# Ordering VectorE's copies behind GpSimd's DMA issues in a planned attention and MoE kernel

## The chip, the cores and the metric

The kernel runs on one core of one Trainium2 chip. The metric is the device time of one execution in microseconds (us). The kernel before takes 302.99 us, the median of three runs (302.73 to 303.19).

The engines are named as in the profile: PE is TensorE, with PEld for its weight loads; ACT is ScalarE; DVE is VectorE; POOL is GpSimd; SP is SyncE, which issues DMAs only. GpSimd issues DMAs too.

## The reference

Sliding-window attention over 8 batches, 8 heads, 576 positions and 64 dimensions, followed by one gated feed-forward layer over the 4608 tokens that come out of it.

```python
scores = scale * np.matmul(q, k.transpose(0, 1, 3, 2))
rel = pos[:, None] - pos[None, :]
mask_plain = (rel >= 0) & (rel < 32)                         # heads 0 to 3
mask_dil = (rel >= 0) & (rel < 32 * 4) & (rel % 4 == 0)      # heads 4 to 7
...
attn_out = np.matmul(attn, v)                                # (8, 8, 576, 64)
x = attn_out.transpose(0, 2, 1, 3).reshape(4608, 512)
h = x @ w_in                                                 # w_in: 512 x 2048
g = h * (1.0 / (1.0 + np.exp(-beta * h)))
out = g @ w_out                                              # w_out: 2048 x 512
```

## The kernel before

**The work.** Tokens go through the feed-forward layer in nine tiles of 512. For a tile t, `slot_h` makes one "slot" for each of 16 column blocks of w_in: four matmuls of 512 columns into one PSUM bank (L887), a tanh on ScalarE (L896) and a gate on VectorE that writes `g` (L901). In tile 0, the first four slots are taken apart, so that the halves of x can come at different times. `block` then makes the output of 128 tokens from 16 matmuls against w_out in four parts of four (L922), an evacuation on ScalarE or VectorE (L937, L939) and a store by SyncE (L942).

**Attention** runs batch by batch, between the slots and blocks of the tile before. q and k of the first three batches are loaded into `st` (L394) and transposed on TensorE (L469 for the dilated heads, L479 for the plain ones), and copied out of PSUM (all copies have line L243). From batch 3 on, GpSimd casts them to DRAM and SyncE's DMA transposes bring them in (L460). Scores of the dilated heads are L683, of the tail L652, of the plain heads L747 (L711 from batch 3). ScalarE takes the exponentials (L619) into `ptd`, `ptt` and `pt`; these are multiplied by a mask (L623) on VectorE or GpSimd, except in batch 0, whose masks are added on TensorE (L673, L733, L736). Values are L788 (dilated), L773 (tail) and L804 (plain); VectorE normalises them (L638, L639) into `xdm`, `xdt` and `xsp`. The result is transposed into `xT`, the input of the slots, on TensorE for batches 0 and 1 (L841, L826, L856) and by SyncE's DMA transposes from batch 2 on (L514, L519, L506, L533).

**SBUF copies with a choice of engine.** `halo` fills the first rows of `vp`; `mixed` makes `dkt` out of `dk`; `padded` makes `qt` out of `dq`; `spread` brings v into `vd`. Their deps and engines are given to `plan.op` with an estimated time for each engine.

**What sets the order.** The kernel schedules itself. Every step is an `Op` with the engines that may run it, a time for each, its deps, a due time `vt` and, where it needs PSUM, a `Group` that takes one of eight banks. `Plan.run` keeps a clock for each engine, picks the next op by estimated start and due time, and emits it; so each engine's queue is fixed before the kernel runs, and on the chip each engine works it off in order, waiting on semaphores. `NUDGE` shifts the estimated start of single ops, by their number, in the choice alone. `CAPS` bounds the banks of one kind. Ops that are flagged `sbuf` keep the estimated times of VectorE and GpSimd apart, since they go from SBUF to SBUF:

```python
if o.sbuf:
    at = {e: max(t, port["DVE" if e == "POOL" else "POOL"]) for e, t in at.items()}
```

Where TensorE would be without work by the plan for more than 170 ns (300 ns early on) and a bank is free, `filler` puts a matmul of zeros there (L1035):

```python
if filler is not None and s <= filler_until and free["PE"] + (300 if free["PE"] < COLD else 170) < s:
```

The masks of the plain heads (`mask_n`) and of the dilated heads (`mask_d`), the identities `ident_b` (for the transposes) and `ident_f` (for beta), and `add_d` are made on GpSimd at the head of its queue, among its DMA issues.

Of the kernel before, what the change touches and what calls it, by code (L numbers as in the profile page):

```python
# [17 lines left out]
class Group:  # L18


    def __init__(self, kind):
        self.kind, self.bank, self.users = kind, None, []
        self.read = {}


class Op:
    def __init__(self, engs, fn, deps, vt, acquire, group, dma, lat, halves=False, sbuf=False):
# [12 lines left out]
class Plan:  # L40
# [3 lines left out]

    CAPS = {"h": 3, "p": 4, "o": 2, "z": 4, "a": 8, "s": 5, "w": 6}
    SWITCH = 95
    NUDGE = {9: -400, 35: 400, 78: -150, 90: 150, 103: -900, 156: -900, 164: -60, 191: -60, 208: 150,
        220: 900, 247: -400, 251: 60, 266: -150, 268: -150, 270: -150, 326: 900, 376: 400,
        397: 900, 420: 900, 432: -900, 490: 900, 525: 150, 545: 60, 554: 900, 562: -60, 571: 60,
        574: 150, 1103: -400, 1113: 400}  # L50
    LAT = {"PE": 210, "ACT": 45, "DVE": 45, "POOL": 60, "SP": 0}
    NEAR = {"PE": 40, "ACT": 60, "DVE": 60, "POOL": 60, "SP": 0}

    def __init__(self, banks):
        self.ops, self.banks = [], banks

    def op(self, engs, fn, deps=(), vt=0.0, acquire=None, group=None, dma=0, lat=None, halves=False, sbuf=False):
        acquire = acquire if acquire is None or isinstance(acquire, list) else [acquire]
        o = Op(engs, fn, deps, vt, acquire, group or acquire, dma, lat, halves, sbuf)
        o.bias = self.NUDGE.get(len(self.ops), 0)  # L60
        self.ops.append(o)
        return o

    def run(self, filler=None, filler_until=0.0):
# [12 lines left out]
        n_held = {k: 0 for k in self.CAPS}  # L77
        ends = []
        halves = False
        port = {"DVE": 0.0, "POOL": 0.0}  # L80

        def release(now):
# [18 lines left out]
        while n_left:  # L101
            best = None
            near = {}
            for o in avail:
                base = o.ready
                at = {e: max([free[e], base] + [t for x, t in o.group.read.items() if x != e]
                             if o.group is not None and e != "PE" else [free[e], base]) for e, d in o.engs}
                if o.sbuf:
                    at = {e: max(t, port["DVE" if e == "POOL" else "POOL"]) for e, t in at.items()}
                fin = min(at[e] + d for e, d in o.engs)  # L110
                for e, d in o.engs:
                    start = at[e]
                    if start + d > fin + 100:
                        continue
                    if o.dma and len(lanes[e]) >= 8:
                        start = max(start, lanes[e][-8])
                    if o.acquire is not None:
                        start = bank_at(o.acquire, start)
                        if start is None:
                            continue  # L120
                    near.setdefault(e, []).append((start, o, d))
            picks = []
            for e, c in near.items():
                first = min(s + o.bias for s, o, _ in c)
                s, o, d = min((x for x in c if x[0] + x[1].bias <= first + self.NEAR[e]), key=lambda x: (x[1].vt, x[0]))
                picks.append((s, o.vt, e, o, d))
            assert picks, "no work can start"
            s, _, e, o, d = min(picks, key=lambda x: (x[0], x[1]))
            if filler is not None and s <= filler_until and free["PE"] + (300 if free["PE"] < COLD else 170) < s:
                now = free["PE"]  # L130
                open_banks = {x.bank for x in held.values()}
                spare = [b for b, t in bank_free.items() if b not in open_banks and t <= now]
                if spare:
                    filler(max(spare, key=lambda b: -bank_free[b]))
                free["PE"] = now + (225 if now < COLD else 115)
                halves = False
# [48 lines left out]
def kernel(  # L185
# [34 lines left out]
    DIRECT = 3  # L220
# [21 lines left out]
    def copy(e, out, in_):  # L242
        (nc.scalar.copy if e == "ACT" else E[e].tensor_copy)(out=out, in_=in_)  # L243
# [134 lines left out]
    mask_ops = {}  # L378

    def late_mask(key, ns, fn, vt):  # L380
        mask_ops[key] = plan.op([("POOL", ns)], fn, vt=vt, sbuf=True)
# [25 lines left out]
    def first_keys():  # L407
# [3 lines left out]
                      ap=[[RD * D, 2 * GD], [2 * S * D, 2], [1, RD * D]])  # L411
        o = load("SP", (stage, src), [], -9.1, 576, .41, 400, 1200)
        return [plan.op([("ACT", 175 + .834 * RD * D), ("DVE", 160 + 1.042 * RD * D)],
                        lambda e, x=x: copy(e, std[0][:, x], stage[:, x]), [o], -9.1, sbuf=True) for x in range(2)]

    def direct_vp(b, deps, vt):

# [2 lines left out]
        for hs in ((slice(0, 4),) if b else (slice(0, 2), slice(2, 4))):  # L420
# [5 lines left out]
            def halo(e, hs=hs):  # L426
                copy(e, rows[0:WIN, hs, 1:NI, 0:D], rows[QT:P, hs, 0:NI - 1, 0:D])
            out.append(plan.op([("DVE", 160 + .27 * n * 320), ("POOL", 170 + 1.04 * n * 320)], halo, [o],
                               b - 1 if b else -2.5, sbuf=True))
        return out  # L430

    def direct_vd(b, deps, vt, tdeps=()):
# [104 lines left out]
    def attention(b, ld, names, vts):  # L537
# [43 lines left out]
        o = plan.op([("DVE", 450), ("POOL", 550), ("ACT", 500)], mixed,  # L581
                    (steps["KD0"] + steps["KD1"] if b < DIRECT else ready["D"][0:1]) + war(("dkt", kv)), vt_of["T"] - .01, sbuf=True)
        used(("dk", kv, 0), o)
        used(("dk", kv, 1), o)
        wrote(("dkt", kv))
# [1 line left out]
        for c in range(2):  # L587
            def padded(e, c=c):
# [2 lines left out]
                     dq[kv][rows, :, :, P:].rearrange("p r h u -> p (r h) u"))  # L591
            o = plan.op([("DVE", 250), ("POOL", 500), ("ACT", 290)], padded,
                        (steps["QD0"] + steps["QD1"] if b < DIRECT else ready["D"][1:]) + [fill1] + war(("qt", kv)),
                        vt_of["T"] - .01, sbuf=True)
            used(("dq", kv, 0), o)
            used(("dq", kv, 1), o)
            tail_ready.append(o)
# [7 lines left out]
        def spread(e):  # L605
            copy(e, vd[kv][:, :, :, 0:D], vd16_of[b])
        o = plan.op([("POOL", 1100), ("DVE", 620), ("ACT", 1030)], spread,
                    [ld["vd"][0], (fill3, fill4)[kv]] + war(("vd", kv)), vt, sbuf=True)
        used("vd16" if b < DIRECT else ("st", kv), o)
        wrote(("vd", kv))  # L610
        vdeps["D"] = [o]
# [4 lines left out]
        def exp_and_mask(key, sop, g, vt, n, sc, w, m, tiles):  # L616
# [4 lines left out]
            if b >= ADDED or key == ("T",):  # L621
                def mask(e):
                    E[e].tensor_tensor(out=w(), in0=w(), in1=m(), op=ALU.mult)  # L623
                ex = plan.op([("POOL", 170 + 2.2 * n), ("DVE", 160 + .8 * n)], mask,
                             [ex] + [mask_tail if key == ("T",) else mask_ops["D" if key[0] in (2, 3) else "n"]],
                             vt, sbuf=True)
            wrote(*tiles)
            sdone[key] = ex

# [439 lines left out]
```

## Time and profile before

| | |
|---|---|
| median of three runs | 302.99 us (302.73 to 303.19) |
| the profiled execution's own time | 302.73 us |
| its span | 301.0 us |
| granted clock of TensorE | 0.999 |
| zero matmuls | 67 |
| first w_in matmul (L887) / first w_out matmul (L922) | 17.92 / 37.26 us |
| DMA | 41.98 MB, mean 139 GB/s |

The profile is of one execution. Its busy shares are means over a head of 18 us in which batch 0 is brought up, a middle up to some 92 us in which attention and the feed-forward layer mix closely, and a rest in which TensorE goes from one group of matmuls to the next. In the timeline, a row merges instructions that follow each other on one engine; the first number is its start, the second its length, both in us, and a bracket at its end holds the engine's idle time before it with what ended it. Rows that begin a new group of matmuls can overlap the last of the group before, because the drain of a matmul is counted in. In the table of windows, an entry is the busy time of an engine in that stretch with the number of instructions in brackets.

### The profile page before, as it was taken

The numbers are of one execution on the slowest core, as the hardware profiler recorded it, in microseconds if no ns is written. First come the engines' busy times: TensorE is split into PE (matmuls) and PEld (weight loads), VectorE is DVE, ScalarE is ACT, GpSimd is POOL, SyncE is SP. The second block draws the span as 40 slices with busy tenths as digits, with TensorE's granted clock in tenths as the row PEclk, the third lists the DMA queues.
The fourth block names the chain that finished last, engine by engine and source line by source line (L and its number), as shares of the span: only waits on it lengthen the run. The fifth ranks groups of instructions, "written<-read, shape, count | busy, mean of one in ns | idle before, by whom it ended". The sixth has DMA issues, their size and how long they took to land.

```text
span 301.0 us, 6071 instructions
## 1 busy us (share of the span) xinstructions
PE 295.5 (98%) x2344; PEld 150.4 (50%) x2344; DVE 187.5 (62%) x424; ACT 172.2 (57%) x311; POOL 83.9 (28%) x121
## 2 busy tenths in 40 slices
PE   8999999999999999999999999999999999999995
PEld 5866546444554445544444544444454444444454
DVE  4769787798857846887677647865772363343300
ACT  3868764867745744667484548454852654554311
POOL 8997324764236006400730074000000000000000
PEclk9999999999999999999999999999999999999999
DMA  8999999899889998999899979993124100100122
GB/s 164 188 210 201 206 178 222 122 133 145 196 188 197 158 199 173 199 158 191 145 172 158 224 146 173 179 211 90 37 74 117 70 1 35 37 35 35 59 82 70
DMA packets 111248, 41.98 MB, mean 139 GB/s; under 512 B 87620, under 2 KB 104596, under 8 KB 111220
## 3 DMA queue, kind: packets, MB, share of 16 engines
q0 software_dynamic: 60336, 18.58, 59.5%
q1 hardware_dynamic: 50740, 22.95, 37.8%
q8 instruction: 18, 0.29, 0.4%
q14 instruction: 10, 0.08, 0.1%
q10 hardware_dynamic: 144, 0.07, 0.1%
HBM read 37.76 MB, written 18.87 MB: 188 GB/s over the span
## 4 chain that ended last, share of the span: by engine, by line
PE 94%; DVE 2%; ACT 1%; POOL 1%; issue 1%; POOLq 0%; ACTq 0%
PE bank L922 41%; PE bank L887 40%; PE bank L804 2%; PE bank L1035 2%; PE bank L683 1%; PE bank L788 1%; PE bank L711 1%; PE bank L469 1%; PE bank L747 1%; PE bank L479 1%; ACT ptd L619 1%; PE bank L773 1%; DVE xdm L639 1%; PE bank L673 1%; DVE ptd L623 1%
## 5 line engine op out<-in xcount | busy, mean ns | idle before, releaser
L922 PE MATMUL bank<-w_out_bf,g 128*128 128x512 bf16 (+2 forms) x608 | 140.0, 368 | 0.0
L901 DVE SCALAR_TENSOR_TENSOR g<-tnh,bank 128x512 bf16<-128x512 bf16 x144 | 97.3, 685 | 68.2 <-ACT tnh L896 67.2
L896 ACT ACTIVATE tnh<-bank,beta_half 128x512 bf16<-128x512 f32 x144 | 97.9, 690 | 70.3 <-PE bank L887 63.8
L887 PE MATMUL bank<-xT,w_in_bf 128*128 128x512 bf16 (+1 forms) x584 | 137.0, 376 | 0.0
L887 PEld LDWEIGHTS <-w_in_bf 128*128 128x128 bf16 x584 | 55.7, 98 | 62.8 <-issue 0.3
L922 PEld LDWEIGHTS <-g 128*128 128x128 bf16 x608 | 54.5, 98 | 55.7
L937 ACT ACTIVATE osb<-bank 128x512 f32<-128x512 f32 (+1 forms) x35 | 20.6, 589 | 31.3 <-PE bank L922 30.7
L619 ACT ACTIVATE pt<-bank 128x384 bf16<-128x384 f32 (+1 forms) x54 | 20.8, 467 | 6.8 <-PE bank L711 4.3
L619 ACT ACTIVATE ptd<-bank 128x512 bf16<-128x512 f32 x32 | 16.8, 602 | 6.2 <-PE bank L683 6.2
L639 DVE TENSOR_TENSOR xsp<-bank,rcp 96x384 bf16<-96x384 f32 x32 | 17.7, 554 | 1.3 <-DVE rcp L638 0.2
L623 DVE TENSOR_TENSOR pt<-pt,mask_n 128x384 bf16<-128x384 bf16 (+1 forms) x41 | 14.8, 391 | 5.7 <-ACT pt L619 5.5
L638 DVE RECIPROCAL rcp<-bank 128x4 f32<-128x4 f32 (+2 forms) x72 | 12.8, 178 | 5.5 <-PE bank L804 2.4
L1001 POOL COPY pace<-xT 1x2 bf16<-1x2 bf16 x4 | 0.7, 175 | 51.2 <-DMA xT<-x 51.2
L394 POOL DMA_DIRECT2D vp<-in_v_dram x9 | 14.7, 1632 | 0.4 <-PE bank L469 0.4
L623 DVE TENSOR_TENSOR ptd<-ptd,mask_d 128x512 bf16<-128x512 bf16 x27 | 12.0, 465 | 3.6 <-ACT ptd L619 3.0
L639 DVE TENSOR_TENSOR xdm<-bank,rcp 128x256 bf16<-128x256 f32 x32 | 13.6, 425 | 1.1
L394 POOL DMA_DIRECT2D s<-in_q_dram x10 | 13.5, 1351 | 0.0
L394 POOL DMA_DIRECT2D vt<-in_v_dram x16 | 13.3, 993 | 0.0
L1035 PE MATMUL bank<-zero 128*128 128x256 bf16 x67 | 11.6, 310 | 1.3 <-DVE warm L302 1.1
L394 POOL DMA_DIRECT2D s<-in_k_dram x10 | 11.0, 1100 | 1.4 <-issue 1.1
L804 PEld LDWEIGHTS <-pt 128*128 128x128 bf16 x192 | 8.9, 97 | 4.7
L804 PE MATMUL bank<-vp,pt 128*128 128x65 bf16 x192 | 9.8, 193 | 0.0
(112 smaller groups left out, 172.2 us busy)
## 6 DMA issues: line engine op xcount, KB each, us to landing
out_dram<-osb SPq DMA_DIRECT2D x35, 256.0 KB
s<-in_k_dram POOLq DMA_DIRECT2D x10, 288.0 KB, 7.1
s<-in_q_dram POOLq DMA_DIRECT2D x10, 288.0 KB, 10.0
w_out_bf<-in_moe_w_out_dram POOLq DMA_DIRECT2D x2, 1024.0 KB, 16.5
vp<-in_v_dram POOLq DMA_DIRECT2D x7, 288.0 KB, 17.3
st<-in_q_dram POOLq DMA_DIRECT2D x6, 288.0 KB, 11.1
x<-xsp SPq DMA_DIRECT2D x12, 144.0 KB
st<-in_k_dram POOLq DMA_DIRECT2D x5, 288.0 KB, 13.2
```

Source lines behind the costliest of these rows:

```text
L394: {"POOL": nc.gpsimd, "SP": nc.sync}[queue].dma_start(out=out, in_=in_)
L619: nc.scalar.activation(out=w(), in_=sc(), func=ACT.Exp, scale=SCALE)
L623: E[e].tensor_tensor(out=w(), in0=w(), in1=m(), op=ALU.mult)
L638: nc.vector.reciprocal(out=r, in_=p[..., D])
L639: nc.vector.tensor_tensor(out=dst, in0=p[..., 0:D], in1=r.unsqueeze(len(p.shape) - 1).to_broadcast(list(p.shape[:-1]) + [D]), op=ALU.mult)
L804: nc.tensor.matmul(pv[:, a, h2, :], lhsT=lhs, rhs=vp[kv][:, (2 * x + h2) * NI + 3 * j + a, 0:D + 1], start=True, stop=True)
L887: nc.tensor.matmul(bank(g)[:, a:z], lhsT=w_in_bf[:, kt, fb * P:(fb + 1) * P], rhs=xT[:, kt, xo + a:xo + z], start=(i == 0 and kt == kts[0] ...
L896: nc.scalar.activation(out=th[:, 0:n], in_=bank(g)[:, 0:n], func=ACT.Tanh, scale=beta_half[:, fb:fb + 1])
L901: nc.vector.scalar_tensor_tensor(out=g_t[t % 2][:, fb, c0:c0 + n], in0=th[:, 0:n], scalar=1.0, in1=bank(g)[:, 0:n], op0=ALU.add, op1=ALU.mult)
L922: nc.tensor.matmul(bank(g)[:, lo:hi], lhsT=g_t[t % 2][:, fb, tb * P:(tb + 1) * P], rhs=w_out_bf[:, fb, lo:hi], start=(fb == 0), stop=(fb = ...
L937: nc.scalar.mul(out=ob[:, lo:hi], in_=bank(g)[:, lo:hi], mul=0.5)
L1035: nc.tensor.matmul(BANKS[b][:, 0:256], lhsT=zero[:, 0:P], rhs=zero[:], start=True, stop=True)
```

## The change

In `Plan.run`, an op with the flag `sbuf=2` may start on VectorE, by the plan, only 300 ns after the end of the last DMA issue that GpSimd was given. The flag goes to the four SBUF copies (`halo`, `mixed`, `padded`, `spread`). The masks, the casts of the first keys and the making of the masks keep the old treatment with `sbuf=1`. Two times of VectorE in the plan become shorter: `mixed` 360 instead of 450 ns, and a mask 160 + 0.53 n instead of 160 + 0.8 n. The table `NUDGE` is another one, with 31 entries instead of 29, none of them shared but for the number 90 (-900 instead of 150) and 420 (-400 instead of 900). No op, no dep and no wait is added in the program itself; what differs is the order in which the ops are emitted, the engine that each op with a choice goes to, the bank that it gets and the number of zero matmuls, 58 instead of 67.

```diff
-    NUDGE = {9: -400, 35: 400, 78: -150, 90: 150, 103: -900, 156: -900, 164: -60, 191: -60, 208: 150,
-        220: 900, 247: -400, 251: 60, 266: -150, 268: -150, 270: -150, 326: 900, 376: 400,
-        397: 900, 420: 900, 432: -900, 490: 900, 525: 150, 545: 60, 554: 900, 562: -60, 571: 60,
-        574: 150, 1103: -400, 1113: 400}
+    NUDGE = {3: -900, 11: 150, 16: -400, 32: -400, 37: -400, 48: 900, 61: 150, 90: -900, 115: 900,
+        155: -150, 195: -400, 240: 900, 293: -150, 323: -400, 333: 400, 354: -150, 360: 60,
+        365: -900, 374: -400, 402: 400, 420: -400, 540: -900, 542: -400, 546: -150, 547: 400,
+        578: -900, 680: 400, 681: 900, 821: -900, 836: 900, 870: 150}
...
+        issuing = 0.0
         port = {"DVE": 0.0, "POOL": 0.0}
...
+                if o.sbuf == 2 and "DVE" in at:
+                    at["DVE"] = max(at["DVE"], issuing)
                 if o.sbuf:
                     at = {e: max(t, port["DVE" if e == "POOL" else "POOL"]) for e, t in at.items()}
...
             if o.sbuf:
                 port[e] = s + d
+            elif o.dma and e == "POOL":
+                issuing = s + d + 300
...
-        o = plan.op([("DVE", 450), ("POOL", 550), ("ACT", 500)], mixed,
+        o = plan.op([("DVE", 360), ("POOL", 550), ("ACT", 500)], mixed,
...
-                ex = plan.op([("POOL", 170 + 2.2 * n), ("DVE", 160 + .8 * n)], mask,
+                ex = plan.op([("POOL", 170 + 2.2 * n), ("DVE", 160 + .53 * n)], mask,
...
```

More of the change, by code (lines that the diff above doesn't have):

```diff
@@ L26, with __init__ @@
 class Op:
-    def __init__(self, engs, fn, deps, vt, acquire, group, dma, lat, halves=False, sbuf=False):
+    def __init__(self, engs, fn, deps, vt, acquire, group, dma, lat, halves=False, sbuf=0):
         self.halves, self.sbuf = halves, sbuf
@@ L55, in __init__, with op @@
         self.ops, self.banks = [], banks
-    def op(self, engs, fn, deps=(), vt=0.0, acquire=None, group=None, dma=0, lat=None, halves=False, sbuf=False):
+    def op(self, engs, fn, deps=(), vt=0.0, acquire=None, group=None, dma=0, lat=None, halves=False, sbuf=0):
         acquire = acquire if acquire is None or isinstance(acquire, list) else [acquire]
@@ L380, in late_mask @@
     def late_mask(key, ns, fn, vt):
-        mask_ops[key] = plan.op([("POOL", ns)], fn, vt=vt, sbuf=True)
+        mask_ops[key] = plan.op([("POOL", ns)], fn, vt=vt, sbuf=1)
     late_mask("D", 2600, lambda e: band(mask_d[:], [[0, 4]], [(1, P)], 0, WIN - 1, 1.0, 0.0), -7.215)
@@ L413, in first_keys @@
         return [plan.op([("ACT", 175 + .834 * RD * D), ("DVE", 160 + 1.042 * RD * D)],
-                        lambda e, x=x: copy(e, std[0][:, x], stage[:, x]), [o], -9.1, sbuf=True) for x in range(2)]
+                        lambda e, x=x: copy(e, std[0][:, x], stage[:, x]), [o], -9.1, sbuf=1) for x in range(2)]
     def direct_vp(b, deps, vt):
@@ L428, in direct_vp @@
             out.append(plan.op([("DVE", 160 + .27 * n * 320), ("POOL", 170 + 1.04 * n * 320)], halo, [o],
-                               b - 1 if b else -2.5, sbuf=True))
+                               b - 1 if b else -2.5, sbuf=2))
         return out
@@ L580, in mixed @@
             copy(e, dkt[kv], dk[kv][:, :, :, CT - KTL:].rearrange("p r h k -> p h k r"))
-        o = plan.op([("DVE", 450), ("POOL", 550), ("ACT", 500)], mixed,
-                    (steps["KD0"] + steps["KD1"] if b < DIRECT else ready["D"][0:1]) + war(("dkt", kv)), vt_of["T"] - .01, sbuf=True)
+        o = plan.op([("DVE", 360), ("POOL", 550), ("ACT", 500)], mixed,
+                    (steps["KD0"] + steps["KD1"] if b < DIRECT else ready["D"][0:1]) + war(("dkt", kv)), vt_of["T"] - .01, sbuf=2)
         used(("dk", kv, 0), o)
@@ L593, in attention @@
                         (steps["QD0"] + steps["QD1"] if b < DIRECT else ready["D"][1:]) + [fill1] + war(("qt", kv)),
-                        vt_of["T"] - .01, sbuf=True)
+                        vt_of["T"] - .01, sbuf=2)
             used(("dq", kv, 0), o)
@@ L607, in attention @@
         o = plan.op([("POOL", 1100), ("DVE", 620), ("ACT", 1030)], spread,
-                    [ld["vd"][0], (fill3, fill4)[kv]] + war(("vd", kv)), vt, sbuf=True)
+                    [ld["vd"][0], (fill3, fill4)[kv]] + war(("vd", kv)), vt, sbuf=2)
         used("vd16" if b < DIRECT else ("st", kv), o)
@@ L623, in mask @@
                     E[e].tensor_tensor(out=w(), in0=w(), in1=m(), op=ALU.mult)
-                ex = plan.op([("POOL", 170 + 2.2 * n), ("DVE", 160 + .8 * n)], mask,
+                ex = plan.op([("POOL", 170 + 2.2 * n), ("DVE", 160 + .53 * n)], mask,
                              [ex] + [mask_tail if key == ("T",) else mask_ops["D" if key[0] in (2, 3) else "n"]],
-                             vt, sbuf=True)
+                             vt, sbuf=1)
             wrote(*tiles)
```

## The prediction

> **What bounds the kernel now.** I read the page first, then the zero matmuls by stretch, then the timeline around every hole that TensorE (PE) shows, then the DMA issues.
>
> From the page (busy time, chain, group, DMA issue):
>
> ```profile
> PE 295.5 (98%) x2344; PEld 150.4 (50%) x2344; DVE 187.5 (62%) x424; ACT 172.2 (57%) x311; POOL 83.9 (28%) x121
> PE 94%; DVE 2%; ACT 1%; POOL 1%; issue 1%; POOLq 0%; ACTq 0%
> ...
> L1035 PE MATMUL bank<-zero 128*128 128x256 bf16 x67 | 11.6, 310 | 1.3 <-DVE warm L302 1.1
> ...
> w_out_bf<-in_moe_w_out_dram POOLq DMA_DIRECT2D x2, 1024.0 KB, 16.5
> ```
>
> PE is the bound: busy 98%, 94% of the chain. So an edit is worth only what it takes out of PE's queue or out of PE's waits. The granted clock is 0.999 throughout, so matmuls have fixed prices: four of 512 columns take 0.863 us (the chain's pieces), 1152 of them 248.6 us in any order. What can change is work that computes nothing (67 zero matmuls) and waits.
>
> Busy time of the zero matmuls alone, by stretch (up to the first w_in slot, the first w_out block, the end of batch 1, two more):
>
> ```profile
> 1.13:17.92 16.79, 9.41 (x53) 5.43 (x53) 1.00 1.27 193
> 17.92:37.26 19.34, 1.66 (x12) 0.99 (x11) 1.00 1.25 206
> 37.26:54.07 16.81, 0.49 (x3) 0.29 (x3) 1.00 1.55 201
> 54.07:90.80 36.73, 0.00 (x0) 0.00 (x0) 1.00 1.26 155
> ```
>
> All slack of this kind lies before 43 us. A warm zero matmul costs 0.109 us (eight lie between 24.49 and 25.36); the first 17 cost 0.213 us each.
>
> The timeline's two holes, at 41.4 to 42.9 and at 61.4 to 64.7:
>
> ```profile
> 41.43 0.29 PE L788 MATMUL bank<-vd,ptd 128*128 128x65 bf16 x4
> 41.77 0.38 PE L841 MATMUL bank<-ident_b,xdm 128*128 128x128 bf16 x4
> 42.31 0.49 PE L1035 MATMUL bank<-zero 128*128 128x256 bf16 x3 [0.16 <-DVE xdm L639]
> 42.86 0.38 PE L841 MATMUL bank<-ident_b,xdm 128*128 128x128 bf16 x4
> ...
> 61.39 1.55 DVE L623 TENSOR_TENSOR ptd<-ptd,mask_d 128x512 bf16<-128x512 bf16 x1 [0.55 <-ACT ptd L619]
> 61.51 2.42 POOL L623 TENSOR_TENSOR ptd<-ptd,mask_d 128x512 bf16<-128x512 bf16 x1
> 62.86 1.23 DVE L623 TENSOR_TENSOR ptt<-ptt,mask_t 96x256 bf16<-96x256 bf16 x1
> 64.69 0.28 PE L788 MATMUL bank<-vd,ptd 128*128 128x65 bf16 x4 [0.73 <-DVE xdm L639]
> ```
>
> First hole: both L841 transposes wait for VectorE's (DVE) norms; from 41.43 to 43.08 PE does 4 + 4 + 4 small matmuls worth 0.56 us, so 1.09 us is lost, zeros included. Second: GpSimd (POOL) masks a ptd tile for 2.42 us; the two DVE masks beside it take 1.55 and 1.23 us where the same shapes take 0.43 and 0.28 us with POOL quiet. DVE loses 2.1 us, and PE idles 0.73 us plus 0.16 us of restart: 0.9 us.
>
> The last views: the first w_out load, and the head of GpSimd's queue.
>
> ```profile
> 35.98 0.63 POOL L394 DMA_DIRECT2D st<-in_q_dram  x1 [1.79 <-DMA w_out_bf<-in_moe_w_out_dram]
> 37.26 1.90 PE L922 MATMUL bank<-w_out_bf,g 128*128 128x512 bf16 x8
> ...
> 5.13 1.74 PE L673 MATMUL bank<-add_d,ident_b 128*128 128x512 bf16 x4 [0.19 <-POOL add_d L345]
> 8.92 0.10 POOL masks.py:197 MEMSET ident_f<- 16x16 f32 x1
> 9.36 0.78 POOL L394 DMA_DIRECT2D w_in_bf<-in_moe_w_in_dram  x1
> ```
>
> The first half of w_out lands between 35.2 (issue 18.84 plus 16.4) and 35.98 us, when POOL is let go by it. DMA is saturated from 4 to 50 us at some 200 GB/s and both kernels issue the same transfers in the same order up to there, so it lands then in the changed kernel too.
>
> **The change part by part.** No operation is added or removed except zero matmuls; the rule, the durations and the nudges only change the emitted order. I compared the two orders engine by engine.
>
> *Head, to the first w_in slot.* GpSimd makes ident_f before ident_b: 0.44 us (8.92 to 9.36), so add_d and the first useful matmul move from 5.13 to 5.57. The memset of `zero` goes behind six small memsets (0.48 us), under that same wait. Two zeros fewer stand before the first transposes (-0.21), then 30 instead of 34 up to the first slot (-0.44), and half-array blocks there go from 6 to 5. Such a block costs 0.10 us going in and 0.12 us coming out (after 37.26 eight matmuls end at 38.99, L747 starts at 39.09; its six, 0.12 us, are done at 39.21, L922 starts at 39.33): -0.21. Sum -0.4, if data are ready. But ScalarE (ACT) takes the vd copy (0.64 us for 576 columns makes some 1.1 for 1024), dkt (0.55) and one more xT copy for fewer q and k copies: about 1 us more on ACT, whose xT copies release the first slot, now near 17.7 instead of 17.92. I take -0.2, bounds -0.4 and +0.5.
>
> *First w_out block.* It is moved ahead of the last three w_in slots: 12 fewer L887 matmuls and six more L747 (0.02 each) before it, -2.47 us; zeros of that stretch go from 11 to 10, -0.1. PE would reach it at 37.26 - 2.47 - 0.2 - 0.1 = 34.5 and wait for w_out until 35.2 to 36.0: +0.7 to +1.5, taken +1.1. Behind it in PE's queue stand all remaining slots. Anything late before it (VectorE's qT copy frees slot 11's bank late, by my count 0.6 us) only uses up this wait. Net with the two terms above: +0.8.
>
> *Hole at 41.4.* All 16 value matmuls now come together, and the two transpose groups each stand behind a slot or a w_out block. Four norms take 4 x 0.55 = 2.2 us on VectorE; between values and first transpose lie a slot and a block, 1.73 us, then another block before the second. No zero matmul is left there: -1.1, bounds -1.1 and 0.
>
> *Hole at 61.4.* Batch 2 has all ptd masks on VectorE; GpSimd gets a ptt mask (0.67 us at 78.93) and one pt mask, and six groups of four matmuls instead of three separate scores from values. -0.9, bounds -0.9 and 0.
>
> *Batch 4.* Here a ptd mask does go to GpSimd, where before had none. VectorE's ptt mask falls into its 2.42 us, and the tail values (L773) wait for that mask after three w_out blocks (2.6 us). Counting from the scores: ScalarE's third exp ends at 2.1, the mask at 4.5; PE wants the tail at 3.7. +0.6, bounds 0 and +0.9, the price of the same pattern at 61.4.
>
> *Copies ordered behind GpSimd's issues.* Of six VectorE copies that lie over an issue in before, the vd copy at 12.19 takes 0.414 us, against 0.419 us at 38.20 with none: VectorE pays nothing. The issue takes 0.92 instead of 0.78 us: 0.15 us on GpSimd, hidden under a saturated DMA. So the rule itself buys nothing on PE; value 0, bounds -0.1 and +0.1. *The Trainium skill, "SBUF — State Buffer", section "Who interferes with whom", says that a VectorE copy in a 2-port mode blocks GpSimd outright, and that an operation with two SBUF inputs contends with a GpSimd operation that reads SBUF, the first to issue keeping the port. By it the waits belong on the masks, which this change leaves out; it would make the batch 4 term the full 2 us on VectorE, but the mask at 61.39 had started first and still took 1.55 us, so the row decides.*
>
> *Half-array blocks after the head*: 21 become 20, -0.2. *From 228 us on* both run w_in and w_out groups back to back: 0.
>
> Sum: 0.8 - 1.1 - 0.9 + 0.6 - 0.2 = -0.8 us. The profiled execution took 302.73 us (span 301.0, 1.7 around it), the lowest of three; the median 302.99 is 0.26 above. 302.73 - 0.8 + 0.26 = **302.2 us**.
>
> **The rivals.**
>
> *SyncE's chain becomes late (slower).* The first cast for batch 3 waits for a gate that VectorE now runs behind the batch 2 vd copy, whose data land near 55: issue at some 56.8 instead of 54.91, 1.9 us later. SyncE's transposes follow in one line (59.91, 62.20, 66.96, 76.68), then xsp and the xT transposes, and before's slot at 91.2 already waited 0.2 us. If all moves by 1.9 us, PE waits that long: 302.2 + 1.9 = 304.1. It decides once xT lands after about 90.0. Against it: the q cast is issued ahead of vp, and the last norms of batch 2 come earlier by about 2 us. 0.25.
>
> *The holes only move (no change).* ScalarE and VectorE set the rate from 26 to 54 us; what closes at 42 and 64 opens before it as waits for banks, as many as 0.8 us. 303.0. 0.25.
>
> *The w_out wait and batch 4 both stay hidden (faster still)*: 302.2 - 1.1 - 0.6 + 0.2 = 300.7. Needs w_out before 34.6, against the row at 35.98. 0.08.
>
> The forecast itself: 0.42.
>
> **How the numbers follow.** About 0.2% (0.6 us) can be told from no change: below 302.4 faster, above 303.6 slower. The forecast's own bounds: low -1.3 (w_out wait 0.7, batch 4 at 0, some 0.2 less in the head), high +0.9 (either hole stays): 301.0 to 303.1. Faster: 0.37 of the forecast, 0.02 of the no-change case, 0.08 of the third: 0.47. Slower: 0.22 of the first rival, 0.05 from the second: 0.27. Same: 0.26. The range reaches to the first rival: 301.0 to 304.1.
>
> **What would show it.** Right: 58 zero matmuls; the first slot near 17.7; PE idle before the first L922 until 35.2 to 36.0, with w_out as releaser; no hole near 42 and 62; DVE masks in batch 4 (near 111) of over 1 us, with a short PE wait at L773. Wrong: the first L922 without a wait, a PE wait over 1 us near 90 whose releaser is xT's transpose, or new waits for banks between 26 and 54 us that add up to more than 1 us.

## The result and the profile after

The changed kernel takes 306.06 us, the median of 20 runs (303.50 to 309.72); the kernel before, in turns on the same chip, 303.00 us (302.69 to 303.53). The ratio is 1.0084, with a 95% interval from 1.0064 to 1.0103: slower by 0.8%. It is smaller than the quotient of the two medians (1.0101), because it leaves out the three slowest runs of the changed kernel (308.09 and above), in which the mean granted clock of TensorE was 0.993 or 0.994. The forecast was 302.2, and its range ended at 304.1. The runs also scatter over 6 us where the kernel before stays within 0.9. The profiled execution took 306.21 us (span 304.5, against 302.73 and 301.0).

The page after, parts that were shown of before (busy time, chain, zero matmuls):

```profile
PE 295.8 (97%) x2335; PEld 150.6 (49%) x2335; DVE 186.8 (61%) x418; ACT 171.4 (56%) x309; POOL 87.9 (29%) x129
PE 74%; DMA 12%; DVE 4%; POOL 4%; SPq 1%; issue 1%; ACT 1%; DVEq 0%; ACTq 0%
...
L1040 PE MATMUL bank<-zero 128*128 128x256 bf16 x58 | 10.2, 319 | 1.7 <-DVE warm L307 1.5
```

TensorE (PE) is busy for as long as before, with 1.4 us less in zero matmuls. But its share of the chain falls from 94% to 74%, and 12% of the chain is now DMA, which had none: PE has begun to wait for data.

Zero matmuls by stretch, cut at the same events (first w_in slot, first w_out block, then the same times as before):

```profile
1.13:20.79 19.66, 8.80 (x48) 5.06 (x48) 1.00 1.25 195
20.79:38.83 18.04, 1.43 (x10) 0.90 (x10) 1.00 1.27 205
38.83:54.07 15.24, 0.00 (x0) 0.00 (x0) 1.00 1.59 198
```

The first slot comes at 20.79 instead of 17.92, and the first w_out block at 38.83 instead of 37.26, although 2.47 us of matmuls fewer stand before it. Compared with its own work, TensorE is thus some 4 us behind at 38.83; the two closed holes bring back about 2 us later, and new waits after 80 us take about 1.3 us. That makes the 3.5 us by which the span has grown. The head's timeline, and below it the three places where PE waits after 80 us:

```profile
17.29 2.09 DVE L248 COPY vp<-vp 32x640 bf16<-32x640 bf16 x2
17.33 0.84 POOL L346 MEMSET mask_n<- 128x864 bf16 x1
...
19.43 0.65 PE L809 MATMUL bank<-vp,pt 128*128 128x65 bf16 x16 [1.32 <-DVE vp L248]
...
20.54 0.90 POOL L399 DMA_DIRECT2D w_out_bf<-in_moe_w_out_dram  x1
...
59.70 0.31 POOL L1006 COPY pace<-g 1x2 bf16<-1x2 bf16 x1 [2.99 <-DVE g L906]
...
81.93 0.56 DVE L248 COPY vp<-vp 32x1280 bf16<-32x1280 bf16 x1 [1.25 <-DMA vp<-in_v_dram]
83.00 0.30 PE L793 MATMUL bank<-vd,ptd 128*128 128x65 bf16 x4 [0.34 <-DVE ptd L628]
...
114.93 0.49 DVE L248 COPY vp<-vp 32x1280 bf16<-32x1280 bf16 x1 [1.22 <-DMA vp<-in_v_dram]
...
144.42 0.48 DVE L248 COPY vp<-vp 32x1280 bf16<-32x1280 bf16 x1 [3.91 <-DMA vp<-in_v_dram]
```

Two things are to be seen. At 17.29 the two halo copies of batch 0 take 1.05 and 1.11 us; before, at 12.64 and 14.78, the same copies took 0.39 and 0.32 us. They lie beside the making of mask_n on GpSimd (POOL), and PE's value matmul stands behind them. This is called the meeting below. And at 81.93, 114.93 and 144.42 VectorE (DVE) stands in its queue before a halo copy whose data have not landed; the ptd masks are queued behind it, and PE waits for them. (The row at 59.70 is batch 3's gate: a tiny copy by which GpSimd waits for the feed-forward layer before it issues that batch's loads.) From the starts of the matmuls (a wait counted with the restart, so longer than the bracket) these three cost 0.51, 0.47 and 0.33 us, and with 0.23 us at 164.5 it is 1.54 us after 80 us; the kernel before loses 0.20 us there.

### The profile page after: what moved, and what is told of

Its sections match the earlier page's. It is cut to its first block, busy times and chain, and to the rows that moved or that the text cites. A ratio compares the mean times of both kernels' runs of the same rounds, so it can differ in the third digit from the quotient of the medians.

```text
span 304.5 us, 6060 instructions
## 1 busy us (share of the span) xinstructions
PE 295.8 (97%) x2335; PEld 150.6 (49%) x2335; DVE 186.8 (61%) x418; ACT 171.4 (56%) x309; POOL 87.9 (29%) x129
## 4 chain that ended last, share of the span: by engine, by line
PE 74%; DMA 12%; DVE 4%; POOL 4%; SPq 1%; issue 1%; ACT 1%; DVEq 0%; ACTq 0%
PE bank L927 33%; PE bank L892 31%; DMA vp<-in_v_dram 6%; DMA dq<-s 4%; POOL s L399 2%; PE bank L1040 2%; DMA xT<-x 2%; PE bank L809 1%; DMA x<-xsp 1%; PE bank L793 1%; SPq L465 1%; POOL vt L399 1%; PE bank L474 1%; PE bank L688 1%; PE bank L716 1%
## 5 line engine op out<-in xcount | busy, mean ns | idle before, releaser
L942 ACT ACTIVATE osb<-bank 128x512 f32<-128x512 f32 (+1 forms) x31 | 18.2, 586 | 35.1 <-PE bank L927 35.0
L628 DVE TENSOR_TENSOR pt<-pt,mask_n 128x384 bf16<-128x384 bf16 (+1 forms) x40 | 13.4, 359 | 4.3 <-ACT pt L624 4.0
L944 DVE TENSOR_SCALAR osb<-bank 128x512 f32<-128x512 f32 (+2 forms) x7 | 4.2, 596 | 17.5 <-PE bank L927 17.5
L628 POOL TENSOR_TENSOR pt<-pt,mask_n 128x288 bf16<-128x288 bf16 (+1 forms) x6 | 4.9, 817 | 34.7 <-ACT pt L624 34.7
L628 DVE TENSOR_TENSOR ptd<-ptd,mask_d 128x512 bf16<-128x512 bf16 x27 | 10.7, 421 | 2.6 <-ACT ptd L624 2.2
L809 PEld LDWEIGHTS <-pt 128*128 128x128 bf16 x192 | 8.9, 97 | 6.5 <-issue 1.8
L1040 PE MATMUL bank<-zero 128*128 128x256 bf16 x58 | 10.2, 319 | 1.7 <-DVE warm L307 1.5
```

Of the source, the lines that this page charges most:

```text
L809: nc.tensor.matmul(pv[:, a, h2, :], lhsT=lhs, rhs=vp[kv][:, (2 * x + h2) * NI + 3 * j + a, 0:D + 1], start=True, stop=True)
L942: nc.scalar.mul(out=ob[:, lo:hi], in_=bank(g)[:, lo:hi], mul=0.5)
L1040: nc.tensor.matmul(BANKS[b][:, 0:256], lhsT=zero[:, 0:P], rhs=zero[:], start=True, stop=True)
```

## Experiments

For most of them the order is pinned: `Plan.run` no longer plans but replays the list of (op, engine, banks) that the kernel had emitted, and `MOVES` shifts single ops in it, so that nothing else moves.

```diff
-    def run(self, filler=None, filler_until=0.0):      # plans
+    SEQ = "..."          # every step as the kernel emitted it: op number, engine, banks
+    MOVES = [(12, "after", 29)]
+    def run(self, filler=None, filler_until=0.0):      # replays SEQ after MOVES
```

Ratios are to the kernel before on the same chip. Kernels of one group ran in turns on one chip; the groups were on different ones.

| kernel | median us (runs) | range | ratio, 95% interval |
|---|---|---|---|
| no_wait | 305.55 (6) | 304.48 to 305.72 | 1.0070, 1.0052 to 1.0088 |
| halo_early | 305.21 (6) | 304.30 to 307.19 | 1.0074, 1.0046 to 1.0102 |
| mask_n_late | 304.43 (12) | 302.98 to 306.77 | 1.0059, 1.0036 to 1.0083 |
| halo_behind | 302.69 (12) | 301.84 to 304.92 | 0.9998, 0.9978 to 1.0018 |
| wait_alone | 313.48 (4) | 313.09 to 314.32 | 1.0354, 1.0336 to 1.0371 |
| table_alone | 303.89 (7) | 303.43 to 304.40 | 1.0028, 1.0018 to 1.0039 |
| before_two | 302.37 (12) | 301.77 to 303.70 | 0.9986, 0.9974 to 0.9999 |
| best_try | 302.81 (12) | 302.22 to 306.48 | 1.0014, 0.9988 to 1.0040 |
| gate_early | 304.98 (6) | 303.87 to 305.78 | 1.0056, 1.0039 to 1.0074 |
| best_gate | 303.29 (12) | 302.57 to 306.42 | 1.0016, 0.9997 to 1.0036 |
| two_behind | 302.37 (12) | 301.71 to 303.38 | 0.9977, 0.9967 to 0.9987 |
| collide | 304.12 (12) | 303.24 to 308.16 | 1.0029, 1.0015 to 1.0043 |
| after_again | 306.09 (12) | 302.81 to 310.73 | 1.0069, 1.0036 to 1.0102 |
| halo_behind_2 | 304.52 (12) | 302.40 to 306.45 | 1.0050, 1.0024 to 1.0075 |

**The parts of the change.** no_wait is the changed kernel without the wait:

```diff
-                if o.sbuf == 2 and "DVE" in at:
-                    at["DVE"] = max(at["DVE"], issuing)
```

> The changed kernel without the two lines that make VectorE's copies wait for GpSimd's issues in the plan; table, estimates and the rest stay. By the plan batch 0's halo copies come at 13.6 and 14.5 us instead of 16.3 and 16.6, batch 1's vd copy goes back to VectorE, batch 3's halo copy goes back to GpSimd, and batch 3's gate comes 2.4 us earlier. Theory A (the waits of the plan push copies beside GpSimd's own work and ahead of late data): no wait of 1.3 us at L809 near 18, first slot near 18.0 instead of 20.80, halo copies 0.32 to 0.39 us each, time 301.0 to 302.5. Rival B (the table of nudges costs it: mask_n ahead of w_out, the first w_out block ahead of three slots, batch 3 late): the waits stay about as they are and the time is 305 or more.

305.55: theory A missed. The first halo copy is back at 0.32 us. The second takes 1.11 us, and PE waits 0.9 us for it:

```profile
14.57 1.11 DVE L246 COPY vp<-vp 32x640 bf16<-32x640 bf16 x1
...
14.89 0.64 POOL L397 DMA_DIRECT2D st<-in_q_dram  x1
...
15.73 0.28 PE L807 MATMUL bank<-vp,pt 128*128 128x65 bf16 x4 [0.88 <-DVE vp L246]
...
16.23 0.84 POOL L344 MEMSET mask_n<- 128x864 bf16 x1
```

It has ended before mask_n begins: nothing but DMA issues lies beside it. At 60.46 it happens again: a qt copy takes 1.76 us over three issues (0.18 us elsewhere), and PE waits at 61.5. At 113.2 a halo copy stands ahead of the masks (1.2 us), as in the changed kernel. So taking the wait out plans another order, which loses as much in other places. wait_alone has the wait with the old table and the old estimates, table_alone the new table with neither:

> The kernel before with the wait of VectorE's copies for GpSimd's issues alone (old table, old estimates). In its emitted order there are 95 zero matmuls instead of 67, batch 0's halo copies come 9 us later by the plan, the vd copies of batches 1 and 2 go to ScalarE and GpSimd, batch 3's halo copy goes to VectorE, and its gate stands behind 40 blocks of PE's matmuls instead of 38. Theory A (waiting for issues gains nothing, and pushing the copies costs): slower than 306, by 28 zero matmuls of 0.109 us (3.1 us) and more behind late data; 307 to 314. Rival B (the table is what costs; the wait is neutral): 302.5 to 304.

> The kernel before with the new table of nudges alone. 55 zero matmuls; the halo copies of batch 0 are back at 13.6 and 14.5 by the plan, on VectorE; the vd copies of batches 1 and 2 stay on VectorE and the halo copy of batch 3 on GpSimd, as in the kernel before; but the making of mask_n comes even ahead of batch 1's last q load. Theory A: what falls beside mask_n's making decides the head; the second halo copy probably does, as in the run without the wait (1.11 us, PE waiting 1.05), so 303.5 to 305.5. Rival B: the table alone gives the changed kernel's time, 305.5 or more. If the table carried the gain and the wait the loss, it would be 301 to 302.5.

The wait alone costs 10.5 us (batch 3's gate at 68.5 instead of 54.8), the table alone 0.9; with both, and the two shorter estimates, 3.1. The parts do not add up. Read from the other side, no_wait and table_alone differ only in the two estimates, and their intervals lie apart (1.0070 against 1.0028), while the wait on top of table and estimates changes nothing clear of noise (1.0084 against 1.0070). Which of the three parts costs the 3.1 us can thus not be said; the runs below look at places in the emitted order instead.

**Batch 0's halo copies.** halo_early moves the copies away from mask_n, mask_n_late moves mask_n away from the copies, collide holds mask_n over them:

```diff
+    MOVES = [(23, "after", 48), (25, "after", 83)]     # halo_early: halos behind qT's copy, behind the second norm
+    MOVES = [(12, "after", 29)]                        # mask_n_late: mask_n behind the first w_out issue
+    MOVES = [..., (12, "before", 199)]                 # collide: halo_behind, and mask_n ahead of the last q load
```

> The changed kernel with its order pinned and two instructions of VectorE moved in it: batch 0's halo copies stand behind qT's second copy and behind the second norm, instead of both behind the tail's mask. Theory A: they take 0.32 to 0.39 us instead of 1.05 and 1.11, the wait of 1.32 us at L809 is gone, the first slot starts near 19.4 instead of 20.80, and the time is lower by 1.3 to 1.5 us, about 304.7. Rival C (the copies are slow because their data land late or because DMA writes the same tile): they take about 1 us wherever they stand, the wait moves, and the time stays within 0.5 us of 306.1.

> The changed kernel with its order pinned and one step of GpSimd moved: the making of mask_n comes behind the issue of the first half of w_out instead of ahead of it; the halo copies stay where they are on VectorE, now over GpSimd's issues. Theory A (a copy from SBUF to SBUF on VectorE is held while GpSimd computes in SBUF, not while it issues DMAs): the same two copies take 0.32 to 0.45 us each, the wait at L809 falls from 1.32 us to under 0.3, time about 304.7. Rival C: they stay at about 1 us and so does the time. w_out is issued 3.2 us earlier, which should not show, since the first w_out block comes at 38.8 and the data at 36.3.

> The kernel halo_behind (runs near 302.4 and near 304.3) with the making of mask_n moved ahead of batch 1's last q load on GpSimd, so that batch 0's halo copies on VectorE always lie beside it. Theory A (the second mode is that the copies, 16.5 to 17.3 in one run and 17.3 in another, meet mask_n's making, which starts at 17.3 to 18.0): all runs in the slow mode, copies of 0.8 to 1.1 us each, the first slot 1.0 to 2.0 us later than the 18.64 of halo_behind, time 303.8 to 305. If the second mode is the DMA chain: 302.4 and 304.3 mixed as before.

In halo_early the copies take 0.35 and 0.32 us, and the first slot comes at 19.04. mask_n_late is the cleaner test, since the copies have not moved in VectorE's order. Its timeline, and collide's under it:

```profile
17.07 0.56 DVE L229 COPY vp<-vp 32x640 bf16<-32x640 bf16 x2
...
19.09 1.03 PE L873 MATMUL bank<-xT,w_in_bf 128*128 128x512 bf16 x4
...
20.84 0.84 POOL L327 MEMSET mask_n<- 128x864 bf16 x1
```

```profile
16.39 0.93 POOL L327 MEMSET mask_n<- 128x864 bf16 x1
16.92 1.61 DVE L229 COPY vp<-vp 32x640 bf16<-32x640 bf16 x2
17.39 0.96 POOL L328 TENSOR_SCALAR_AFFINE_SELECT mask_n<-mask_n 128x864 bf16<-128x864 bf16 x1
...
18.58 0.65 PE L790 MATMUL bank<-vp,pt 128*128 128x65 bf16 x16 [0.68 <-DVE vp L229]
...
19.94 1.03 PE L873 MATMUL bank<-xT,w_in_bf 128*128 128x512 bf16 x4
```

In the same place the copies take 0.32 and 0.31 us without GpSimd beside them; with it 0.57 and 1.11, and the first slot is 1.30 us later than in halo_behind's 18.64. Rival C (late data) falls. The times follow less neatly than the mechanism: halo_early and mask_n_late, both without the meeting, still have runs above 306, so something else scatters. And collide's median, 304.12, lies between the two of halo_behind (302.69 and, further down, 304.52), all on different chips; the cost of the meeting is read from the profiles alone.

**The halo copies of later batches.**

```diff
+    MOVES = [(531, "after", 568), (671, "after", 704), (811, "after", 850)]   # behind the dilated norms
```

> The changed kernel with its order pinned and three instructions of VectorE moved: the halo copies of batches 3, 4 and 5 stand behind the norms of the dilated values instead of ahead of the ptd masks. Theory A (in VectorE's queue the masks stand behind a copy that waits for vp's landing, 1.25, 1.22 and 3.91 us): PE's waits of 0.51, 0.47 and 0.41 us at L793 near 82, 115 and 145 are gone, the time falls by 1.2 to 1.5 us to about 304.7, and the runs scatter by less than 1 us instead of 6, since the landing is off the path. Rival D (the whole chain of batch 3 is late, xT and the plain values too): the waits come back at L809 or at a slot as long as before, time and scatter as in the changed kernel.

302.69, 1.7 lower than mask_n_late on the same chip, and the waits near 82, 115 and 145 are gone: in its profile PE loses 0.18 us after 80 us. The copy waits for nothing there (84.18, 116.50, 145.20), and the plain values that need it come later. The intervals of the two ratios (up to 1.0018, and from 1.0036) lie apart. The time is lower than forecast (304.7), and the scatter (3.1 us) does not shrink to 1.

**Is it the gate?** gate_early lets batch 3's loads go behind the last gate product of tile 0; best_try collects the moves, and best_gate adds the gate:

```diff
-    ... g_t[b % 2][0:1, 0, 0:2]        gop[b - 2, 0]
+    ... g_t[0][0:1, NFB - 1, 0:2]      gop[0, NFB - 1]
+    MOVES = [(32, "after", 7), (12, "after", 29), ..., (951, "after", 990), (1091, "after", 1130)]   # best_try
```

> The changed kernel with its order pinned and one dependency exchanged: the gate of batch 3's loads waits for the last gate product of tile 0 (slot 15) instead of the first of tile 1, so GpSimd can start the casts right behind its dkt copy, some 3 us before the 59.70 of the changed kernel; the v loads behind it still wait for TensorE's transposes and come some 1.5 us earlier. Theory E (the loss from 80 us on is the DMA chain from batch 3's gate on, which runs late against TensorE; the halo copy is only the place where it is felt): half or more of the waits of 0.51, 0.47 and 0.41 us near 82, 115 and 145 go, 304.0 to 305.2. If only the place in VectorE's queue counts (the landing follows TensorE, not the gate): 305.5 to 306.5.

> The changed kernel with its order pinned and these moves: halo copies of batches 3 to 7 behind the dilated norms (batches 3 to 5 gave 302.69), mask_n's making behind the first w_out issue (so that batch 0's halo copies never lie beside it), ident_f behind add_d (0.44 us that the first useful matmul came later). Theory A: the two modes of the runs with the halo copies behind (302.4 and 304.2) become one, the first slot starts near 18.3, 301.6 to 302.3, no run above 303. If the second mode has another cause than the copies beside mask_n, runs of 304 remain.

> The kernel best_try with the same exchange at batch 3's gate. In the profile of best_try TensorE waits 0.34, 0.66 and 0.58 us for xT, dq and xT near 145, 168 and 205, all at the end of SyncE's chain. Theory E: with the chain 1.5 to 3 us earlier these waits go, the runs above 303 vanish and the median is 301.3 to 302.2. If each batch's chain finds its own pace, whatever the start, the waits return by batch 5 or 6 and the time is that of best_try, 302.2 to 303.0 with a tail to 306.

The gate came 5 us earlier (54.7), the wait at 82 went, but those at 113.8 (0.38), 144.4 (1.07) and later stayed, and best_gate is no faster than best_try. But the exchange has a side effect in both kernels. It brings GpSimd's issues under batch 2's vd copy, which took 0.42 us at 58.17 in the changed kernel. In gate_early:

```profile
55.97 1.67 POOL L380 DMA_DIRECT2D s<-in_k_dram  x1
...
56.26 1.82 DVE L229 COPY vd<-vd 128x1024 bf16<-128x1024 bf16 x1
...
58.72 1.02 PE L873 MATMUL bank<-xT,w_in_bf 128*128 128x512 bf16 x4 [0.37 <-DVE g L887]
```

PE loses 0.56 us there by the starts of its matmuls, and 0.55 us in best_gate. In best_gate's one profile no wait of over 0.13 us is left after 80 us, where best_try's has three, all at the end of a DMA (xT, dq, xT), of 1.58 us together. So theory E is not refuted: an earlier gate may help late and cost at 58. What is shown to help is the copy's place.

**The two holes on which the gain rested, closed in the order of before.**

```diff
+    ENGINES = {397: "DVE"}                                 # batch 2's ptd mask of GpSimd
+    MOVES = [(174, "before", 274), (180, "before", 277)]   # two w_out blocks ahead of the two transposes; 3 zeros out
+    MOVES += [(671, "after", 708), (811, "after", 850), (951, "after", 990), (1091, "after", 1130)]   # two_behind
```

> The kernel before with its order pinned and only the two holes closed on which the prediction's gain rested: batch 2's ptd mask of GpSimd goes to VectorE at its place (61.5), and the two transposes at 41.8 and 42.9 each stand behind a w_out block that came right after them, with the three zero matmuls between them taken out. By the prediction's steps: minus 0.9 and minus 1.1, 301.0. Bounds: if the second half of w_out has not landed by 41.8 (issue at 25.71 and 16.4 us make 42.1), PE waits 0.3 to 0.9 there and the time is 301.3 to 301.9. If waits for banks take the place of the holes, 302.5 to 303.0.

> The kernel before_two (the kernel before with only the two holes closed; 302.37, its profile 303.70 with a wait of 1.09 us at 112.2 for a ptd mask behind the halo copy) with the halo copies of batches 4 to 7 behind the dilated norms on VectorE. Theory E: that wait goes and the time is 301.3 to 301.9; what is left of the two holes' 2.0 us shows up. If xT, dq or the plain values are as late as vp, the wait moves there and the time stays 302.2 to 302.5.

before_two gains 0.57 of the 2.0 us. Its timeline shows where the rest went:

```profile
42.30 1.02 PE L908 MATMUL bank<-w_out_bf,g 128*128 128x512 bf16 x4 [0.63 <-DMA w_out_bf<-in_moe_w_out_dram]
...
45.37 0.28 PE L733 MATMUL bank<-qT,kT 64*128 64x96 bf16 x5 [0.59 <-ACT xT L229]
...
112.53 0.48 DVE L229 COPY vp<-vp 32x1280 bf16<-32x1280 bf16 x1 [4.34 <-DMA vp<-in_v_dram]
...
113.53 0.30 PE L774 MATMUL bank<-vd,ptd 128*128 128x65 bf16 x4 [0.92 <-DVE ptd L609]
```

The second half of w_out lands at 42.3: behind the hole at 41.4 stood a DMA, and 0.63 us of it could not be won in this order. Then a bank is late (0.59), and at 112 PE, now earlier, meets vp's landing. two_behind takes that last wait away and has the lowest ratio of all, 0.9977 (0.9967 to 0.9987), though the interval of before_two (0.9974 to 0.9999) overlaps it. It missed its 301.3 to 301.9; in its profile xT is then 0.8 us late at 145.9.

**What scatters.** Six profiles of the changed kernel's own order, all but the first pinned (after_again timed too), and halo_behind a second time:

> The changed kernel's order, pinned, nothing moved: a second profile. Theory A + E (two causes that add): a run's time is about 302.4 us, plus 1.3 to 2.0 if batch 0's halo copies lie beside mask_n's making (first slot near 20 to 21 instead of 18.2 to 18.7), plus the waits of TensorE for vp, xT or dq after 80 us (0.5 to 3). If one cause carries all of it, the time goes with the first slot alone or with the late waits alone.

> A third profile of the same program, to be read in the same way: first slot between 18.2 and 20.8, waits after 80 us between 0.5 and 3 us, and their sum giving the time within 0.5 us.

> A fourth profile of the same program, to be read in the same way: first slot between 18.2 and 20.8, waits after 80 us between 0.5 and 3 us, and their sum giving the time within 0.5 us.

> A fifth profile of the same program, to be read in the same way: first slot between 18.2 and 20.8, waits after 80 us between 0.5 and 3 us, and their sum giving the time within 0.5 us.

> The changed kernel's order, pinned, timed in turns with the next kernel on one chip. If the chip makes no difference: near 306. If the four single runs stand for the program: 303.5 to 304.5 here. Either way its excess over the kernel halo_behind should be what TensorE waits at L793 behind the halo copies, 1.0 to 2.3 us in the five profiles.

> The kernel halo_behind again, beside the changed kernel's order on the same chip. Theory A + E: 1.0 to 2.3 us under it, and 302.2 to 303.0 itself. If its gain of 3.4 us was the chip's, the two lie within 0.5 us.

| profile | halo copies, us | first slot | waits after 80 us | its time |
|---|---|---|---|---|
| changed kernel | 1.05, 1.11 | 20.79 | 1.54 | 306.21 |
| after_2 | 0.36, 0.30 | 18.61 | 2.32 | 304.44 |
| after_3 | 0.32, 0.31 | 18.88 | 1.12 | 303.57 |
| after_4 | 0.32, 0.31 | 18.61 | 1.10 | 303.35 |
| after_5 | 0.32, 0.31 | 18.92 | 1.67 | 304.06 |
| after_again | 0.32, 0.31 | 19.29 | 1.86 | 304.55 |
| halo_behind | 0.41, 0.30 | 18.64 | 0.18 | 302.20 |
| halo_behind_2 | 1.69, 1.11 | 20.96 | 0.55 | 306.45 |

(The waits are gaps over 0.13 us between matmul starts; gaps of just one matmul, where its record is missing, are left out.) 302.4 plus the late waits gives the four single profiles within 0.3 us, as expected. In the same order on every engine, the copies meet mask_n in one profile of six and in one of two. Their own start does not decide it: in after_again they start at 17.27 and escape, in halo_behind_2 the first starts at 16.74 and is held. In the two profiles with the meeting, mask_n starts at 17.33 and 17.42; in the six others at 17.59 to 18.41.

The profiles put the halo copies' place at 1.1 to 2.3 us (the waits after 80 us) against 0.2 to 0.6 with the copies behind. The pair on one chip, medians of 306.09 and 304.52, fits that, but does not show it: by the ratios, 1.0069 and 1.0050, it is 0.6 us, and their intervals overlap. halo_behind_2 itself missed its 302.2 to 303.0. In its profile the head is the reason: the meeting there cost more than the wait. PE's clock (fourth entry) in halo_behind_2, by microsecond, and the wait ahead of it:

```profile
19.52 0.65 PE L790 MATMUL bank<-vp,pt 128*128 128x65 bf16 x16 [1.96 <-DVE vp L229]
```

```profile
19.00:20.00 1.00, 0.48 (x16) 0.47 (x16) 0.93 (x3) 0.13 (x1) 0.93 (x2) 1.00 1.11 215
20.00:21.00 1.00, 0.82 (x18) 0.68 (x15) 0.93 (x4) 0.21 (x1) 0.94 (x4) 0.80 1.14 213
21.00:22.00 1.00, 0.78 (x5) 0.41 (x4) 0.97 (x4) 0.40 (x1) 1.00 (x2) 0.50 1.09 207
...
23.00:24.00 1.00, 1.00 (x7) 0.45 (x5) 0.00 (x0) 0.40 (x1) 0.47 (x1) 0.50 1.20 202
```

(Ahead of the clock: length, then busy time and instructions of PE, PEld, DVE, ACT, POOL.) After 1.96 us without work the granted clock is 0.50 from 20.6 to 24.0 us, and 512 columns take 0.427 instead of 0.216 us: 1.6 us more. After the changed kernel's 1.32 us it stayed at 1.00. Such a stretch makes a run's mean clock 0.993 to 0.995 (3.4 us at half in some 302). Of the 20 runs of the changed kernel five have a mean of 0.993 or 0.994, and they are 306.67 to 309.72; of after_again's 12 five, 306.58 to 310.73; none of the 29 runs of before beside two_behind is under 0.998. That those ten all had this meeting is argued, not shown: they have no trace. A run of best_try, where mask_n comes too late for a meeting, has such a mean too (306.48, 0.994), so another wait can do it.

## Why the prediction was wrong

**The step that failed is "Copies ordered behind GpSimd's issues", valued at 0.** The step priced the issue that the copy no longer overlaps, not the place that the wait sends it to. Batch 0's halo copies went from 12.64 and 14.78 to 17.29, beside GpSimd's own computing and right ahead of L809; those of batches 3 to 5 stand ahead of the ptd masks and wait for vp. The price of the first stood in the prediction itself, at 61.39 (1.55 instead of 0.43 us), but for masks, and it was applied to batch 4's alone; the sum had nothing for either. What they cost: 1.3 us and more in the head where the copies meet mask_n, and 1.1 to 2.3 us after 80 us. The gain side was read from too little, too. The row itself is right (0.414 us over an issue), but other copies do pay over issues alone: 1.11 us in no_wait, 0.61 us in table_alone at 14.81, 1.82 us in gate_early. Even in before, the cast at 5.29 took 0.88 us over two issues, against 0.56 us at 5.39 in the changed kernel. Since no_wait is no faster, what the wait by itself is worth stays open.

The Trainium skill, "SBUF — State Buffer", section "Who interferes with whom", says that a single-input copy in a 2-port mode and a GpSimd operation shut each other out, and that the one that issues first keeps the ports; the prediction used the half of it in which VectorE is first. The rows agree with the other half in the main: beside mask_n the copies take 0.57 to 1.69 instead of 0.31 us. But at 17.29 the copy's record begins 0.03 us ahead of the memset's, and it was held all the same.

**Head, -0.2 (-0.4 to +0.5).** Measured +2.87 in the profile, and +0.7 to +1.4 in the five profiles of the same order where the copies escape, so outside the bounds in all six. add_d came nearly as forecast (5.48, against 5.57). Not priced were a bank that a norm frees late (PE waits 0.37 us at L741) and the meeting, 1.3 us in collide, 2.3 and 1.6 more at half clock in halo_behind_2.

**First w_out block, +0.8.** Both kernels do issue the same transfers in the same order up to there, as the prediction says, but not at the same time: mask_n's making goes ahead of the first w_out issue, 20.54 instead of 18.84. The data still came only 0.3 us later (GpSimd is let go by them at 36.29 instead of 35.98). The wait did not come, since PE was later (38.83); in gate_early, with the first slot at 18.24, it does, 0.3 us. The 0.6 us counted for slot 11's bank came at 35.39 as 0.53, uncovered. And PE waits 0.30 us at 38.83 for xT's copy behind a ptt mask of 1.12 us: the vd copy, sent to GpSimd, lies beside it.

**Holes, -1.1 and -0.9.** Both are gone, as predicted, and the zero matmuls are 58. But closing them in before's order bought 0.57 us (by the interval, 0.0 to 0.8): the worth of a hole was taken as its length, with no look at which landing stands behind it.

**Batch 4, +0.6.** The size came (0.47 at 115.9), the reason did not: GpSimd's ptd mask takes 1.15 us, not 2.42, and VectorE's ptt mask 0.28. VectorE stands before the halo copy. That the size came is luck.

**The rivals.** The slower one was the nearest: late data from batch 3's gate on, priced at 1.9, measured at 1.1 to 2.3. Its gate was put at 1.9 us late and was 4.9 (59.70); in the five profiles of the same order without the meeting it is 2.4 to 3.0 late (57.2 to 57.8), so about half of it is PE's own lateness. Its place was wrong: not xT at 90 but vp, issued behind the q cast and read by a copy that had moved from GpSimd to VectorE, ahead of the masks. The prediction saw vp behind the cast (its issue is now at 65.36, before it was at 59.22) and counted it in favour. No rival had the head, so nothing reached 306.

## What to carry to other kernels

An order that avoids one overlap creates another: follow the deferred instruction to its new place, and price what runs beside it there and what is queued behind it. On an in-order engine, a copy that waits for a DMA belongs behind everything that does not need it; here halo_behind was 1.7 us faster than mask_n_late on the same chip. Taking one part of a change out of a kernel that plans itself yields another order, not the same order without that part; the pinned order is what made single moves readable. Where the bound engine is 98% busy, ask of each hole which landing stands just behind it before counting its length as gain, and when runs scatter, take several profiles of one program.

## What the runs showed of the hardware

In halo_behind_2, a wait of 1.96 us was followed by a stretch of 3.4 us in which TensorE's granted clock was halved. The Trainium skill, "TensorE: Matmul & The Clock Gate", Part 1, puts the fall after an idle window of about 3.4 us; here TensorE was not idle that long, and 1.32 us in the changed kernel was not followed by a fall. The length of one wait is not all that counts: in wait_alone the clock was 0.50 from 36.6 to 40.0 us, after waits of which none was over 0.78 us. In the 3.41 us before the fall TensorE was busy for 1.42 us in halo_behind_2 and for 1.47 us in wait_alone. Where the limit lies, no run here shows.

A held copy ends just behind a GpSimd instruction. Beside mask_n's making, in the changed kernel, collide and halo_behind_2, all six halo copies end 0.18 us after the end of a memset or an affine_select. In the changed kernel and in collide each is held by the one instruction that it meets. In wait_alone a copy that started at 17.33, as one affine_select ended and before the next began, took its usual 0.32 us. In halo_behind_2 the first copy started at 16.74, 0.02 us behind the start of a DMA issue (0.71 us), and ended only with the memset that followed, 1.69 us later.

DMA issues hold a copy in some cases and not in others. Of batch 0's halo copies in the twenty profiles, 19 lie over issues alone. Fifteen took 0.30 to 0.39 us, as long as or little longer than those beside nothing; the four others took 0.46 and 0.51 (two_behind, best_gate), 0.61 (table_alone) and 1.11 us (no_wait). Starting after the issue is not enough to be held: in best_try two copies lie inside one issue (16.79, 0.71 us) and take 0.32 and 0.31 us. What decides it stays open.

It also goes the other way: a VectorE cast of 0.56 us at 5.11 stretched GpSimd's second add_d select from 0.29 to 0.67 us in halo_behind's profile, and with it moved the first useful matmul by 0.4 us.
